# Three exchanges in the written order of a fused attention and token-mixing kernel, with seven PSUM homes moved

## The chip, the cores and the metric

The kernel runs on one core of a Trainium2 chip. A core has five engines that run their own instruction streams and meet only through semaphores: TensorE (PE, matrix products and transposes; PEld is its weight load), VectorE (DVE), ScalarE (ACT), GpSimd (POOL) and SyncE (SP), which here issues every DMA transfer. The metric is the device time of one execution in microseconds. All times inside an execution count from the first instruction of the profiled span.

## The reference

Inputs q, k and v are [8 batches, 8 heads, 576 positions, 64], and there are three weights. A linear attention with cosine and sine weights is followed by a mixing of the tokens:

```python
theta = np.pi / 2.0 * pos / S
def phi(x, c, s):
    r = np.maximum(x, 0.0)
    return np.concatenate([r * c, r * s], axis=-1)
q_p = phi(q, cos_w, sin_w); k_p = phi(k, cos_w, sin_w)
kv = np.einsum('bhsf,bhsd->bhfd', k_p, v)
z = np.sum(k_p, axis=2)
num = np.einsum('bhsf,bhfd->bhsd', q_p, kv)
den = np.einsum('bhsf,bhf->bhs', q_p, z)[..., None] + 1e-06
x = (num / den)                      # heads put side by side: [8, 576, 512]
...
W_tok = scale * np.einsum('bsd,btd->bst', x @ w_q, x @ w_k)
mixed = np.einsum('bst,btd->bsd', W_tok, x)
out = np.maximum(mixed, 0.0) @ w_out
```

## The kernel before

Work is cut into 16 halves: half H is four heads of batch H // 2. Nothing is scheduled by a compiler. One string, `ORDER` (lines 26 to 67), lists all steps as words, and lines 555 to 568 emit them one after the other; each engine gets its own steps in that sequence and works through them strictly in order. A word is a step, its number, sometimes a or b for one part of it, then `:n` for its home, the first of the eight PSUM banks that it writes, or `@A`, `@V`, `@G` for ACT, DVE or POOL. For the evictions OE, `:n` is one of 16 output buffers in SBUF instead.

The steps that matter below, for half H, batch b, row tile i:

- LK, LQ, LV (SP, line 145): load raw k, q, v. RK, RQ (lines 203, 205): relu and cast to bf16. VS (DVE, line 234) or VG (POOL, line 248): v times the cosine and sine table.
- QT H (PE, line 295, nine transposes of 128x128): q turned, into two banks (homes n and n+1). QM H (DVE, line 316, two instructions): the turned q times its table, from PSUM to SBUF; it empties QT's home.
- KV H (PE, line 285, 36 products): k'v; KE empties it into SBUF.
- N g (PE, line 340, 20 products; g is 2H or 2H+1): numerator and denominator from QM and KE, two banks. EP, RC or RJ: the reciprocal. X g (DVE, line 393): the quotient x; it empties N's home.
- XR H (PE, line 419, 20 transposes): x turned, two banks. XE H (line 213 on DVE, 209 on ACT) empties it.
- WK b, WQ b, KX b (PE, lines 439, 452, 466): the small products of the mixing, emptied by KW, QW, XK; XA and XB copy parts of XK's result across partitions.
- MX i (PE, line 489): one quarter of the mixed tokens of a batch, two banks. ME i (line 500 on ACT, 502 on DVE): relu, into SBUF.
- WO i (PE, line 509, four products of 128x512): a row tile of the product with w_out, one bank. OE i (line 209 on ACT, 213 on DVE): from PSUM into an output buffer. ST i (SP, line 519): store.

A step that writes a home waits until whatever stood there has been emptied. So the number after the colon is a dependency: QT12 in home 0 holds banks 0 and 1 until QM12 has read them, and the next step in home 0 waits for QM12. Buffers of most SBUF tiles alternate between two (`rq0`, `rq1`), raw inputs between five. SP works through loads and stores in one queue in the order of the string: a store whose eviction is late holds up the loads written behind it.

Of the kernel before, what the change touches and what calls it, by code (L numbers as in the profile page):

```python
# [39 lines left out]
CV8a@G KX2:7 LV9a KE6@A CW4@G X15 CW2@A N13:2 LK9a CW3@A CW5@V N12:0 EP13@V XR7:4 XK2@V LK8b WO8:6  # L40
RC13 XA2@A X13 EP12@A CV8b@G LK9b XE7@A WO2:7 RC12 VS8 LV11a WO7:2 CV9b@A RQ8a@G X12 OE8:0@A MX8:4
WO6:3 RQ8b@A RK8a@G LQ13a ME8@V OE7:1@A LQ11b XR6:0 RQ9a@G LQ10a WO1:6 CV9a@A XE6@V RQ9b@G LK11b
OE2:2@A WO4:2 LK11a VS9 OE6:3@A LQ11a RK8b@A QT9:0 RK9a@G OE1:4@A WK3:3 LV11b QM9 QT8:4 RK9b@G KW3@A
OE4:5@A KV8:0 QM8 XB2@A KV9:6 ST4 KE8@A LV12a MX9:4 KE9@A MX11:0 VG11a N16:2 ME9@A LK10a ME11@V
WQ3:6 RC16 LQ10b KX3:7 X16 QW3@A MX10:0 LV10a XK3@A N17:4 ME10@A N19:2 RK11@V N18:6 LV10b EP19@A
WO11:0 EP17@V RQ11@A LQ12a RC17 EP18@V X17 WO5:1 VG11b OE11:6@V WO10:4 OE5:5@A RC19 RC18 ST11 X18
WO9:5 LK12a X19 LK10b QT11:6 LQ13b OE9:7@A RQ10@G LV12b KV11:2 XA3@A QM11 XR8:0 LK12b KE11@A XR9:6
VG10a XE8@A QT10:2 LQ12b XE9@V WO0:5 QM10 OE10:8@A MX13:0 OE0:6@A MX12:6 N22:2 WO12:4 RQ13a@G ME12@V
EP22@A LV15a XB3@A ME13@A LV13a RC22 VG10b WK4:5 X22 LQ14b LV14b MX14:0 KW4@A N23:6 ME14@V LQ14a
MX15:2 EP23@A KX4:5 RK10@A LV13b WQ4:0 XK4@V RQ13b@G RC23 WO3:1 ME15@A X23 XA4@G XB4@A QW4@A RQ12b@G  # L50
KV10:2 OE3:9@V RQ12a@A QT13:6 OE12:10@A VG12 MX18:0 WO14:5 QM13 KE10@A ST12 ME18@A LK13b XR11:2
OE14:11@A LK13a MX16:0 N21:6 XE11@V ME16@A LV14a N20:4 EP21@A EP20@V RK12@A QT12:0 RJ10 X21 WO16:2
RQ14b@A X20 WO13:3 QM12 VG13 XR10:4 OE13:10@A MX19:6 KV12:0 ME19@A ST13 WO17:3 OE16:12@A LK15b
KE12@V XE10@V LK14b MX17:0 LK14a OE17:13@A N25:6 ME17@V N24:4 LV15b RQ14a@A WK5:3 ST2 EP25@V EP24@V
RK13@A RJ12 QT14:0 X24 WO21:2 KW5@A X25 CV14a@G KV13:4 OE21:10@A QM14 CV14b@A WQ5:3 ST21 KE13@A
KX5:2 LQ15b VS14 LQ15a XR12:4 XK5@A N27:0 ST3 XE12@A N26:6 LK15a RK14a@G WO20:2 RC26 EP27@V RC27
# [542 lines left out]
```

## Time and profile before

| | |
|---|---|
| time, median of 3 runs | 120.47 us |
| lowest and highest run | 119.94 and 120.84 us |
| profiled execution: span from first to last instruction | 117.9 us (its own time is not listed apart from the three) |
| PE, busy share of the span | 96.3 us, 82% |
| DVE | 91.0 us, 77% |
| ACT | 82.7 us, 70% |
| POOL | 64.8 us, 55% |
| transfers | 39.38 MB, 334 GB/s over the span |
| chain that ended last, by engine | PE 46%, DMA 25%, DVE 9%, SP's queue 8%, ACT 4% |

The shares are averages over stages with different limits. Rows of the timeline give the start, the duration, engine, line and operation, then out<-in by the program's names, the shapes and a count; a bracket at the end is the idle time of the engine before it and who ended it. Consecutive instructions of one line are merged into one row, so four WO in a row show as one row with x16. A row of the chain has a start, a duration and what it was.

### The profile page before, as it was taken

Reading aid. Unit: us, or ns where it says so; the run is one execution under the profiler, and the core shown is the slowest. Engines: PE = TensorE matmul, PEld = TensorE weight load, DVE = VectorE, ACT = ScalarE, POOL = GpSimd, SP = SyncE. Lnnn points to the kernel's source line nnn. Section 1 sums busy time; section 2 is a strip of 40 time slices with the busy share of each in tenths; the row PEclk is TensorE's granted clock in tenths of the full one; section 3 lists DMA queues with packets and bytes.
Section 4 is the critical chain, followed back from the end, with each engine's and each line's share of the span. In section 5 each row is a group of like instructions: output and inputs, shape, how many; then the busy total and the mean of one; then the engine's idle time right before and its main releaser. Section 6 shows DMA issues by size and latency. Waiting matters only on the chain.

```text
span 117.9 us, 4967 instructions
## 1 busy us (share of the span) xinstructions
PE 96.3 (82%) x2109; PEld 65.3 (55%) x2109; DVE 91.0 (77%) x163; ACT 82.7 (70%) x146; POOL 64.8 (55%) x66
## 2 busy tenths in 40 slices
PE   0007866887897879998999889997999999999970
PEld 0006855756676768546966556654784566463420
DVE  2009799699899998989798887796997996794620
ACT  4555578489999797997684769975888783546340
POOL 7600599843435984584599972899549921102000
PEclk9999999999999999999999999999999999999998
DMA  3999999999999999999999899786989456999874
GB/s 95 353 389 408 393 363 351 391 389 396 385 393 389 391 385 387 389 395 384 387 381 341 271 317 379 274 253 215 299 285 321 171 205 268 402 343 402 340 306 172
DMA packets 20662, 39.38 MB, mean 334 GB/s; under 512 B 3232, under 2 KB 3232, under 8 KB 20640
## 3 DMA queue, kind: packets, MB, share of 16 engines
q1 hardware_dynamic: 20640, 39.07, 91.8%
q8 instruction: 16, 0.26, 1.0%
q14 instruction: 6, 0.05, 0.1%
HBM read 29.62 MB, written 9.44 MB: 331 GB/s over the span
## 4 chain that ended last, share of the span: by engine, by line
PE 46%; DMA 25%; DVE 9%; SPq 8%; ACT 4%; issue 3%; POOL 2%; POOLq 0%; DVEq 0%
PE ps L509 23%; DMA kraw<-in_k_dram 11%; DMA vraw<-in_v_dram 9%; SPq L145 8%; DMA qraw<-in_q_dram 5%; DVE qm L316 5%; PE ps L340 4%; PE ps L452 3%; PE ps L466 3%; PE ps L489 3%; PE ps L439 3%; PE ps L285 3%; PE ps L419 2%; PE ps L295 2%; POOL rq L205 2%
## 5 line engine op out<-in xcount | busy, mean ns | idle before, releaser
L248 POOL TENSOR_TENSOR v<-vraw,vtab 128x1152 bf16<-128x1152 f32 (+1 forms) x12 | 35.6, 2976 | 4.5 <-DVE qm L316 2.5
L509 PE MATMUL ps<-wow,mix 128*128 128x512 bf16 x144 | 34.6, 380 | 0.0
L393 DVE TENSOR_TENSOR x<-ps,rec 128x640 bf16<-128x640 f32 x32 | 25.4, 816 | 0.7
L209 ACT COPY o<-ps 128x512 f32<-128x512 f32 x25 | 14.6, 590 | 10.5 <-PE ps L509 9.2
L316 DVE TENSOR_TENSOR qm<-ps,qtab 128x1152 bf16<-128x1152 bf16 x28 | 19.7, 749 | 1.3 <-PE ps L295 1.2
L509 PEld LDWEIGHTS <-mix 128*128 128x128 bf16 x144 | 12.5, 98 | 14.5 <-issue 1.7
L295 PE MATMUL ps<-ident,rq 128*128 128x128 bf16 x126 | 10.3, 232 | 10.9 <-ACT rq L203 10.0
L234 DVE TENSOR_TENSOR v<-vb,vtab 128x2304 bf16<-128x2304 bf16 (+1 forms) x11 | 12.0, 1110 | 7.5 <-ACT vb L209 6.7
L500 ACT ACTIVATE mix<-ps 128x576 bf16<-128x576 f32 x23 | 14.5, 651 | 2.5 <-PE ps L489 2.3
L340 PE MATMUL ps<-kvs,qm 64*128 64x65 bf16 x640 | 14.0, 193 | 2.8 <-DVE qm L316 1.8
L340 PEld LDWEIGHTS <-qm 64*128 64x128 bf16 x640 | 12.6, 96 | 4.9 <-issue 3.3
L295 PEld LDWEIGHTS <-rq 128*128 128x128 bf16 x126 | 8.2, 104 | 12.5 <-issue 9.9
L203 ACT ACTIVATE rk<-kraw 128x1152 bf16<-128x1152 f32 (+1 forms) x14 | 13.9, 995 | 0.5 <-DMA kraw<-in_k_dram 0.3
L211 POOL TENSOR_SCALAR kx<-kx 64x256 bf16<-64x256 bf16 x10 | 4.0, 400 | 15.8 <-ACT kx L209 10.1
L205 POOL TENSOR_SCALAR rq<-qraw 128x576 bf16<-128x576 f32 (+1 forms) x13 | 10.1, 776 | 4.4 <-ACT rk L203 2.6
L211 POOL TENSOR_SCALAR vb<-vraw 128x576 bf16<-128x576 f32 (+1 forms) x7 | 5.7, 809 | 10.8 <-DMA vraw<-in_v_dram 9.5
L285 PE MATMUL ps<-v,rk 64*64 64x130 bf16 x432 | 9.1, 228 | 1.9 <-ACT mix L500 0.7
L209 ACT CAST kvs<-ps 128x260 bf16<-128x260 f32 (+1 forms) x15 | 6.5, 436 | 5.1 <-PE ps L285 3.8
L285 PEld LDWEIGHTS <-rk 64*64 64x64 bf16 x432 | 7.5, 112 | 4.3 <-ACT mix L500 1.3
L502 DVE TENSOR_SCALAR mix<-ps 128x576 bf16<-128x576 f32 x9 | 6.8, 753 | 3.3 <-PE ps L489 3.1
L213 DVE COPY xT<-ps 128x1280 bf16<-128x1280 bf16 (+1 forms) x9 | 7.3, 813 | 2.2 <-PE ps L419 2.0
L203 ACT ACTIVATE rq<-qraw 128x576 bf16<-128x576 f32 (+1 forms) x10 | 8.3, 830 | 0.9 <-DMA qraw<-in_q_dram 0.8
(65 smaller groups left out, 135.0 us busy)
## 6 DMA issues: line engine op xcount, KB each, us to landing
kraw<-in_k_dram SPq DMA_DIRECT2D x32, 288.0 KB, 5.9
qraw<-in_q_dram SPq DMA_DIRECT2D x32, 288.0 KB, 5.9
vraw<-in_v_dram SPq DMA_DIRECT2D x32, 288.0 KB, 5.9
out_dram<-o SPq DMA_DIRECT2D x36, 256.0 KB, 3.0
wof<-in_moe_w_out_dram SPq DMA_DIRECT2D x4, 256.0 KB, 5.7
wkf<-in_moe_w_k_dram SPq DMA_DIRECT2D x1, 128.0 KB, 6.7
wqf<-in_moe_w_q_dram SPq DMA_DIRECT2D x1, 128.0 KB, 6.5
```

What stands on the lines that cost most here:

```text
L203: A.activation(dst, s, AF.Relu)
L205: eng.tensor_scalar(dst, s, FMAX, 0.0, op0=ALU.min, op1=ALU.max)
L209: A.copy(dst, s)
L234: V.tensor_mul(v2_b[H % NV2][:, part, :, :, 0:D], vb_b[H % NPREP][:, part].unsqueeze(3).to_broadcast([P, n, C, 2, D]), vtab.unsqueeze(1).t ...
L248: G.tensor_mul(dst[:, part, :, :, 0:D], s[:, part].unsqueeze(3).to_broadcast([P, n, C, 2, D]), vtab.unsqueeze(1).to_broadcast([P, n, C, 2, ...
L285: nc.tensor.matmul(kv_v[o, r, :], rk_of(H)[a, pr, c, :], v2_b[H % NV2][a, pr, c, :, 0:D + 1], start=(c == 0), stop=(c == C - 1))
L295: nc.tensor.transpose(qt_v[:, c, :], rq_b[H % NPREP][:, c, :, :], ident)
L316: V.tensor_mul(qm_b[H % NQM][:, :, r, 0:C, :], q_t[:, r].unsqueeze(1).to_broadcast([P, 2, C, H2]), qtab)
L340: nc.tensor.matmul(nv[:, pr, u, :], qm_b[H % NQM][a, s, r, 2 * u:2 * u + 2, :], kv_b[H % 2][a, r, pr if H in KV_WIDE else 0, s, 0:D + 1], ...
L393: V.tensor_tensor(x_b[b % NX][:, :, 4 * h:4 * h + 4, :].rearrange("p u (w r) d -> p r w u d", r=2)[:, r], nv[:, :, :, 0:D], rec(g).to_broa ...
L500: A.activation(dst, s, AF.Relu, scale=scale_moe)
L509: nc.tensor.matmul(o, mix_b[bp % 2][:, m, rt * P:(rt + 1) * P], wow[:, m, :], start=(m == 0), stop=(m == NDM - 1))
```

## The change

Only the string changes. Three pairs of steps change places, and seven numbers of homes are new: QT11 6 to 4, WO9 5 to 0, WO10 4 to 1, XR8 0 to 6, XR9 6 to 4, KV12 0 to 6, MX19 6 to 0. The order of the steps on DVE, ACT, POOL and SP stays as it was.

```diff
-OE2:2@A WO4:2 LK11a VS9 OE6:3@A LQ11a RK8b@A QT9:0 RK9a@G OE1:4@A WK3:3 LV11b QM9 QT8:4 RK9b@G KW3@A
+OE2:2@A QT8:4 LK11a VS9 OE6:3@A LQ11a RK8b@A QT9:0 RK9a@G OE1:4@A WK3:3 LV11b QM9 WO4:2 RK9b@G KW3@A
...
-RQ14b@A X20 WO13:3 QM12 VG13 XR10:4 OE13:10@A MX19:6 KV12:0 ME19@A ST13 WO17:3 OE16:12@A LK15b
+RQ14b@A X20 WO13:3 QM12 VG13 XR10:4 OE13:10@A KV12:6 MX19:0 ME19@A ST13 WO17:3 OE16:12@A LK15b
```

The second exchange stands on lines 46 and 47 of the string: `WO5:1 VG11b OE11:6@V WO10:4 OE5:5@A ... WO9:5 ... QT11:6` becomes `WO5:1 VG11b OE11:6@V QT11:4 OE5:5@A ... WO9:0 ... WO10:1`, with XR8 and XR9 on the same line.

First place, TensorE ahead of KV8. The names are bf16 tiles in SBUF: mix_104 the mixed tokens (WO), rq_81 and rq_80 the q of halves 9 and 8 (QT), xT_97 the turned x (WK), rk_78 and v_84 the k and v of half 8 (KV8). A bracket names the engines whose semaphores the instruction waits for. Before:

```order
L509 MATMUL ps<-wow,mix_104 128x512 [waits Activation_49]
...
L295 LDWEIGHTS rq_81 [waits Pool_49]
L295 MATMUL ps<-ident,rq_81 128x128 [waits DVE_49]
...
L439 MATMUL ps<-wkw,xT_97 128x64 [waits Activation_49]
...
L295 LDWEIGHTS rq_80
L295 MATMUL ps<-ident,rq_80 128x128
...
L285 MATMUL ps<-v_84,rk_78 64x130 [waits DVE_49]
```

And after the change:

```order
L295 LDWEIGHTS rq_80 [waits Activation_49,Pool_49]
L295 MATMUL ps<-ident,rq_80 128x128 [waits DVE_49]
...
L295 LDWEIGHTS rq_81 [waits Pool_49]
L295 MATMUL ps<-ident,rq_81 128x128 [waits DVE_49]
...
L439 MATMUL ps<-wkw,xT_97 128x64 [waits Activation_49]
...
L509 MATMUL ps<-wow,mix_104 128x512
...
L285 MATMUL ps<-v_84,rk_78 64x130 [waits DVE_49]
```

WO4 moved from ahead of both q transposes and WK3 to just ahead of KV8, and QT8 took its place.

Second place, TensorE from WO5 to KV11: mix_104 and mix_105 are the two buffers of mixed tokens (WO5 uses 104, WO10 and WO9 use 105), rq_81 is the q of half 11 (QT11), rk_79 and v_85 are KV11's. Before:

```order
L509 MATMUL ps<-wow,mix_104 128x512
...
L509 MATMUL ps<-wow,mix_105 128x512 [waits DVE_49]
...
L295 LDWEIGHTS rq_81 [waits Activation_49]
L295 MATMUL ps<-ident,rq_81 128x128 [waits DVE_49]
...
L285 LDWEIGHTS rk_79 [waits DVE_49]
L285 MATMUL ps<-v_85,rk_79 64x130 [waits Pool_49]
```

And after the change:

```order
L509 MATMUL ps<-wow,mix_104 128x512
...
L295 LDWEIGHTS rq_81 [waits Activation_49]
L295 MATMUL ps<-ident,rq_81 128x128 [waits DVE_49]
...
L509 MATMUL ps<-wow,mix_105 128x512 [waits DVE_49]
...
L509 MATMUL ps<-wow,mix_105 128x512 [waits Activation_49]
...
L285 LDWEIGHTS rk_79 [waits DVE_49]
L285 MATMUL ps<-v_85,rk_79 64x130 [waits Pool_49]
```

QT11 now stands ahead of the two WO, and the second of these waits for an eviction on ACT (bank 1, emptied by OE5). Further on, WO0 has a wait for DVE that it did not have (bank 5, emptied by XE9).

Third place, TensorE from MX19 (kx_102) and KV12 (rk_78, v_84) to MX17 (kx_102 again, behind WO17). Before:

```order
L489 LDWEIGHTS kx_102
L489 MATMUL ps<-wq_100,kx_102 128x288 [waits Activation_49]
...
L285 LDWEIGHTS rk_78 [waits DVE_49,Activation_49]
L285 MATMUL ps<-v_84,rk_78 64x130 [waits Pool_49]
...
L509 MATMUL ps<-wow,mix_105 128x512 [waits Activation_49]
...
L489 MATMUL ps<-wq_100,kx_102 128x288 [waits DVE_49]
```

And after the change:

```order
L285 LDWEIGHTS rk_78 [waits Activation_49]
L285 MATMUL ps<-v_84,rk_78 64x130 [waits Pool_49]
...
L489 LDWEIGHTS kx_102
L489 MATMUL ps<-wq_100,kx_102 128x288 [waits DVE_49]
...
L509 MATMUL ps<-wow,mix_105 128x512 [waits Activation_49]
...
L489 MATMUL ps<-wq_100,kx_102 128x288 [waits Activation_49]
```

KV12 moved ahead of MX19, and the wait for DVE (QM12, which empties home 0) went from KV12 to MX19.

More of the change, by code (lines that the diff above doesn't have):

```diff
@@ L42 @@
 WO6:3 RQ8b@A RK8a@G LQ13a ME8@V OE7:1@A LQ11b XR6:0 RQ9a@G LQ10a WO1:6 CV9a@A XE6@V RQ9b@G LK11b
-OE2:2@A WO4:2 LK11a VS9 OE6:3@A LQ11a RK8b@A QT9:0 RK9a@G OE1:4@A WK3:3 LV11b QM9 QT8:4 RK9b@G KW3@A
+OE2:2@A QT8:4 LK11a VS9 OE6:3@A LQ11a RK8b@A QT9:0 RK9a@G OE1:4@A WK3:3 LV11b QM9 WO4:2 RK9b@G KW3@A
 OE4:5@A KV8:0 QM8 XB2@A KV9:6 ST4 KE8@A LV12a MX9:4 KE9@A MX11:0 VG11a N16:2 ME9@A LK10a ME11@V
 WQ3:6 RC16 LQ10b KX3:7 X16 QW3@A MX10:0 LV10a XK3@A N17:4 ME10@A N19:2 RK11@V N18:6 LV10b EP19@A
-WO11:0 EP17@V RQ11@A LQ12a RC17 EP18@V X17 WO5:1 VG11b OE11:6@V WO10:4 OE5:5@A RC19 RC18 ST11 X18
-WO9:5 LK12a X19 LK10b QT11:6 LQ13b OE9:7@A RQ10@G LV12b KV11:2 XA3@A QM11 XR8:0 LK12b KE11@A XR9:6
+WO11:0 EP17@V RQ11@A LQ12a RC17 EP18@V X17 WO5:1 VG11b OE11:6@V QT11:4 OE5:5@A RC19 RC18 ST11 X18
+WO9:0 LK12a X19 LK10b WO10:1 LQ13b OE9:7@A RQ10@G LV12b KV11:2 XA3@A QM11 XR8:6 LK12b KE11@A XR9:4
 VG10a XE8@A QT10:2 LQ12b XE9@V WO0:5 QM10 OE10:8@A MX13:0 OE0:6@A MX12:6 N22:2 WO12:4 RQ13a@G ME12@V
```

## The prediction

> **What bounds the kernel now.** I read three views in this order: busy time by stretch, the idle places of TensorE from 50 us on, and the chain of waits. The first has, after each stretch, the busy time and instruction count of PE, PEld, DVE, ACT and POOL, then the granted clock, the DMA share and the GB/s.
>
> ```profile
> 31.00:57.30 26.30, 23.59 (x547) 17.63 (x548) 24.70 (x42) 23.11 (x43) 14.94 (x19) 1.00 1.05 389
> 57.30:80.67 23.37, 21.63 (x475) 14.13 (x475) 19.61 (x34) 18.11 (x35) 19.74 (x11) 1.00 0.91 314
> 80.67:114.30 33.63, 33.59 (x633) 19.39 (x633) 25.66 (x44) 20.35 (x38) 12.67 (x12) 1.00 0.84 300
> ```
>
> From 80.67 to 114.30 PE is busy 33.59 of 33.63 us: whatever brings PE to 80.67 earlier ends the kernel earlier, if the other engines and the transfers follow. From 57.30 to 80.67 PE has 1.74 us free. The timeline of PE from 50 to 115 us names an idle place over 0.15 us only four times:
>
> ```profile
> 56.01 1.25 PE L285 MATMUL ps<-v,rk 64*64 64x130 bf16 x72 [0.43 <-DVE qm L316]
> 66.04 0.47 PE L419 MATMUL ps<-ident,x 64*128 64x64 bf16 x20 [0.47 <-DVE qm L316]
> 68.75 0.48 PE L340 MATMUL ps<-kvs,qm 64*128 64x65 bf16 x20 [0.42 <-DVE qm L316]
> 80.67 0.72 PE L285 MATMUL ps<-v,rk 64*64 64x130 bf16 x36 [0.71 <-ACT mix L500]
> ```
>
> These are KV8 (with KV9 behind it), XR9, N22 and KV12, 2.03 us in all. Each waits for a q product (QM9, QM11, QM10, QM12) to leave PSUM or to be ready; the releaser that the last row names is corrected below. The three exchanges lie just ahead of them.
>
> **The change part by part.** No instruction is added or removed, and the order on DVE, ACT, POOL and SP is the same. So I walk PE's new order with start-to-start times from the old one, and let each step wait for what it needs.
>
> *First exchange (QT8 before QT9, WO4 after WK3).* Old rows:
>
> ```profile
> 52.10 1.90 PE L509 MATMUL ps<-wow,mix 128*128 128x512 bf16 x8
> 52.95 1.35 DVE L234 TENSOR_TENSOR v<-vb,vtab 128x2304 bf16<-128x2304 bf16 x1
> 53.83 0.67 PE L295 MATMUL ps<-ident,rq 128*128 128x128 bf16 x9
> 54.34 0.75 PE L439 MATMUL ps<-wkw,xT 128*128 128x64 bf16 x20
> 54.54 2.75 DVE L316 TENSOR_TENSOR qm<-ps,qtab 128x1152 bf16<-128x1152 bf16 x4 [0.24 <-PE ps L295]
> 54.92 0.67 PE L295 MATMUL ps<-ident,rq 128*128 128x128 bf16 x9
> 55.44 0.59 ACT L209 COPY o<-ps 128x512 f32<-128x512 f32 x1
> 57.34 0.42 PE L489 MATMUL ps<-wq,kx 64*128 64x288 bf16 x4
> ...
> out_dram<-o SPq DMA_DIRECT2D x1, 256.0 KB, 4.0
> ```
>
> The first row is WO1 and WO4: (53.83 - 52.10) / 2 = 0.87 each. QT9 takes 0.51 to the next start (54.34 - 53.83), WK3 0.58 (54.92 - 54.34). New: QT8 at 52.97, QT9 53.48, WK3 53.99, WO4 54.57, PE ready for KV8 at 55.44. QT9 ends at 53.48 + 0.67 = 54.15, so QM9 no longer waits for it but only for VS9 on its own engine, which ends at 54.30. DVE instructions in a row start some 0.05 before the last one's end, so QM9 starts at 54.25 instead of 54.54: 0.29 earlier. The fifth row is QM9 and QM8 without a gap; both move by 0.29, to an end at 57.00. KV8, held by QM9, moves by 0.29 to 55.72; MX9, held by QM8 (57.29, its start was 57.34), moves by 0.29 as well. More than 0.29 cannot be had here, because VS9 is now what QM9 waits for.
> What WO4's move costs: OE4 (seventh row) starts at 55.64 instead of 55.44. Behind it on ACT stand XB2 and the drain KE8, which then runs to about 57.0; MX11 needs it at 57.17, so 0.15 of cover is left. On SP the store ST4 and the six loads behind it go 0.20 later. The last row is ST4: 4.0 us from issue to landing, so transfers are queued ahead and 0.20 us is not seen. Cost 0; were the cover gone, 0.2.
>
> *Second exchange (QT11 ahead of WO9 and WO10, four homes changed).* Old rows:
>
> ```profile
> 60.39 3.63 PE L509 MATMUL ps<-wow,mix 128*128 128x512 bf16 x16
> 60.39 1.15 ACT L203 ACTIVATE rq<-qraw 128x1152 bf16<-128x1152 f32 x1
> 62.46 1.56 DVE L393 TENSOR_TENSOR x<-ps,rec 128x640 bf16<-128x640 f32 x2
> 63.86 0.67 PE L295 MATMUL ps<-ident,rq 128*128 128x128 bf16 x9
> 64.56 1.42 DVE L316 TENSOR_TENSOR qm<-ps,qtab 128x1152 bf16<-128x1152 bf16 x2 [0.54 <-PE ps L295]
> 65.10 0.47 PE L419 MATMUL ps<-ident,x 64*128 64x64 bf16 x20
> 65.61 1.23 ACT L209 COPY xT<-ps 128x1280 bf16<-128x1280 bf16 x1
> 66.44 0.68 PE L295 MATMUL ps<-ident,rq 128*128 128x128 bf16 x9
> 66.54 0.82 DVE L213 COPY xT<-ps 128x1280 bf16<-128x1280 bf16 x1 [0.56 <-PE ps L419]
> 66.95 1.03 PE L509 MATMUL ps<-wow,mix 128*128 128x512 bf16 x4
> 67.28 1.41 DVE L316 TENSOR_TENSOR qm<-ps,qtab 128x1152 bf16<-128x1152 bf16 x2
> ```
>
> All of it first moves by the 0.29 just gained, as PE runs without a wait from 57.34 to 66. The first row is WO11, WO5, WO10, WO9: (63.86 - 60.39) / 4 = 0.87. New: WO11 60.10, WO5 60.97, QT11 61.84 (its input RQ11, the second row, is ready at 61.54 - 0.29 = 61.25; its home 4 was left by X17, which ends before X18 starts at 62.46 - 0.29), ending at 62.51. WO9 goes at 62.35, WO10 at 63.22, KV11 at 64.09, XR8 at 64.7. WO9's new home 0 must be drained by OE11, which stands before X18 on DVE and so ended before 62.17: no wait. QM11 now only follows X19 (third row, end 64.02 - 0.29 = 63.73) instead of waiting 0.54 for QT11: it runs 63.68 to 65.10, 0.88 earlier. XR9 in its new home 4 needs it and starts at 65.15 instead of 66.04; PE's idle 0.47 there all but goes, since PE is ready at about 65.05.
> Then a new wait. XR9 fills banks 4 and 5, so WO0 in bank 5 must wait for XE9. XR9 ends at 65.62, XE9 runs 65.66 to 66.48, WO0 starts at 66.53 where PE was ready at 65.15 + 0.40 (66.44 - 66.04) + 0.51 = 66.06: a wait of 0.47, WO0 only 0.42 earlier than 66.95. Queued behind WO0 are MX13, MX12 and N22, and N22 waits for QM10 anyway. QM10 follows XE9 on DVE and moves with it: 66.40 instead of 67.28, 0.88 earlier, ending at 67.81; N22 starts at 67.87 instead of 68.75. PE reaches N22 at 66.53 + (68.75 - 0.42 - 66.95 = 1.38) - about 0.1 = 67.8 at the latest. So the new wait lies beside one that was there, and costs 0. MX13 now also waits for OE10 behind XE8 on ACT: XE8 starts with XR8's end at about 65.25, ends at 66.5, OE10 (0.59, like OE4) at 67.1; MX13 goes at 67.5. Sum at N22: 0.29 + 0.59 = 0.88.
>
> *Third exchange (KV12 ahead of MX19, homes swapped).* Old rows:
>
> ```profile
> 74.34 4.57 POOL L248 TENSOR_TENSOR v<-vraw,vtab 128x2304 bf16<-128x2304 f32 x1 [0.39 <-PE ps L285]
> 79.11 1.41 DVE L316 TENSOR_TENSOR qm<-ps,qtab 128x1152 bf16<-128x1152 bf16 x2
> 79.37 0.47 PE L419 MATMUL ps<-ident,x 64*128 64x64 bf16 x20
> 79.67 0.29 PE L489 MATMUL ps<-wq,kx 64*128 64x288 bf16 x2
> 80.00 0.65 ACT L500 ACTIVATE mix<-ps 128x576 bf16<-128x576 f32 x1
> 80.54 0.58 ACT L209 COPY o<-ps 128x512 f32<-128x512 f32 x1
> 81.32 1.04 PE L509 MATMUL ps<-wow,mix 128*128 128x512 bf16 x4
> 82.40 0.58 ACT L209 COPY o<-ps 128x512 f32<-128x512 f32 x1 [1.27 <-PE ps L509]
> 83.14 0.76 PE L439 MATMUL ps<-wkw,xT 128*128 128x64 bf16 x20
> ```
>
> KV12 sat in home 0, where QT12 had been: it waited for QM12 (second row, end 80.52), not for ME19, which no step of KV12 reads. In old times (the 0.88 comes off all of it): KV12 in home 6 starts after XR10 at 79.67, as v for it (first row, end 78.91) is there, and takes 0.65 (81.32 - 80.67). PE is ready for MX19 at 80.32; home 0 holds it until QM12 ends, start 80.57. WO17 follows about 0.15 later at 80.72 instead of 81.32. ME19 now starts at 80.91 instead of 80.00 and ends at 81.56; OE16 behind it at 82.05, OE17 at 82.54 instead of 82.98. WK5, whose bank OE17 empties, starts at 82.59 instead of 83.14: 0.55. The longer wait of ACT for MX19 takes 0.05 of the 0.60.
>
> *Sum.* 0.29 + 0.59 + 0.55 = 1.43, taken as 1.4. Bounds: QM9's start between 54.25 and 54.40 (an ordinary PE-to-DVE hand-over in place of the back-to-back one) gives 0.29 to 0.14; the third between 0.45 and 0.60. So 1.1 to 1.5 if all is passed on, and 1.4 is nearest to the measured hand-overs.
>
> A rule that speaks against this: the stretch row at 31 us shows 389 GB/s. The Trainium skill, "DMA: Bandwidth & Descriptors", Specifications, puts the HBM limit of a core at about 358 GB/s; by it 26.30 us at 389 would take 28.6 us (an estimate from that page), loads would be late everywhere and the lead worth nothing. The measured 389 GB/s is above that limit, so I do not take it as this run's bound.
> The clock: all three stretches have 1.00. The Trainium skill, "TensorE: Matmul & The Clock Gate", "A second HAM failure mode: psum-queue depth-cycling", says that short idles between groups can drop the clock, by which removing four of them would add to the gain; this case's clock shows no such drop, so I add nothing.
>
> **The rivals.**
>
> ```profile
> 68.66 4.64 DMA vraw<-in_v_dram
> 73.30 0.66 POOL rq L205
> ...
> 79.47 0.59 ACT L209 COPY o<-ps 128x512 f32<-128x512 f32 x1 [0.69 <-PE ps L509]
> ...
> DMA to landing us min/median/max: 2.0/3.0/5.9
> ```
>
> *Loads set the middle.* The chain of waits (first two rows) runs at 68.66 through a load of v into RQ12 on POOL. If that is real, the second exchange's 0.59 is lost there; SP moves by only 0.29, with ST11 behind OE11. Gain 0.29 + 0.55 = 0.84: 119.6. Against it: RQ12 reads q, not v, so the link looks like a coincidence of times.
> *Transfers set the end.* If 300 GB/s is all that the queue yields after 80.67, the last store cannot use the third exchange, and of the rest between 0.29 (SP's gate) and 0.88 passes; middle 0.58: 119.9. For it: stores take 3.0 us to land in the median against 2.0 at best (last row), so a queue stands. Against it: the same queue gave 389. [...]
> *Slower.* OE13 (third row) writes the same slot of o as OE12 and needs ST12 landed. ST12 is issued with OE12's end, 0.88 earlier; if its landing stays, OE13 ends at 79.8, when WO17, whose bank OE13 empties, wants to start (80.72 - 0.88 = 79.84). Each us later holds PE one us, and the loads behind ST13 too. ST12 took 4.0 us (the same row as ST4's). PE is later than before once OE13 ends after 81.27, that is, once ST12 takes some 6.4 us; the worst store took 5.9. Past that point by 1.0: 121.5.
>
> **How the numbers follow.** The median of the three runs is 120.47, the profiled span 117.9, so 2.57 lie around it; the execution's own time is not listed apart. Likeliest: span 116.5, time 120.47 - 1.4 = 119.07, say 119.1, chance 0.60. Loads in the middle 0.17, transfers at the end 0.17, slower 0.06. The range goes from 118.6 (a gain of 1.5, and the 0.4 by which the highest run lies off the median) to 120.1 (past both middle rivals), leaving out the slow one and the rivals' tails. One per cent, about what a measurement can tell from no change, is 1.2 us: 119.27. Of the likeliest case some four fifths lie below it (0.48). Within one per cent: its rest and the two middle rivals, 0.48. Slower by over one per cent: 0.04, most of the slow case.
>
> **What would show it.** First step right: KV8's idle gone or near 0.3, QM9 starting as VS9 ends. Second: QM11 without idle before it, XR9 too, and a new idle of some 0.5 before WO0, released by XE9. Third: KV12 right behind XR10, idle of about 0.2 before MX19, QM12 its releaser. N22 0.9 and WK5 1.4 earlier, PE's end at 112.9 instead of 114.3. Wrong would be: WK5 earlier by 1.4 but the last store not (transfers), or RQ12 unmoved (loads).

## The result and the profile after

The kernel before takes 120.73 us and the changed one 119.13 us (medians of six runs each on one chip). The ratio is 0.9891, with a 95% interval of 0.9857 to 0.9925. In a second set of runs, beside before again, it was 118.91 against 120.29 us, ratio 0.9880 (0.9837 to 0.9924). The change is faster by about 1.1%. Some executions were slower as a whole (121.77 us among the six of before, 189.75 us in the profiled one of the first exchange alone), and the ratios leave such runs out, as this text leaves out that one trace.

The profiled execution of the changed kernel has a span of 117.4 us, only 0.5 less than that of before. So I compare stretches between fixed places in the program: from XR6 to KV8 (first exchange), from KV8 to N22 (second), from N22 to WK5 (third), and on to the end of the last eviction. The columns are those of the prediction's stretches: window, its length, then the busy times. First before, then after, then the same changed kernel profiled a second time (after, again).

```profile
51.70:56.01 4.31, 3.88 (x67) 2.82 (x67) 3.59 (x6) 3.64 (x8) 2.25 (x3) 1.00 1.05 387
56.01:68.75 12.74, 11.77 (x297) 8.22 (x297) 10.95 (x21) 8.72 (x17) 11.18 (x6) 1.00 0.99 344
68.75:83.14 14.39, 13.58 (x333) 8.72 (x333) 11.61 (x19) 11.40 (x23) 11.03 (x6) 1.00 0.86 288
83.14:114.89 31.75, 31.12 (x556) 17.76 (x551) 23.99 (x42) 19.73 (x37) 10.20 (x12) 1.00 0.83 303
```

```profile
52.32:56.50 4.18, 3.83 (x66) 2.73 (x67) 3.67 (x5) 3.54 (x8) 2.53 (x4) 1.00 1.01 346
56.50:68.83 12.33, 11.76 (x294) 8.12 (x296) 10.79 (x20) 8.72 (x17) 8.83 (x5) 1.00 1.02 372
68.83:82.72 13.89, 13.28 (x332) 8.99 (x333) 11.63 (x19) 11.63 (x24) 12.57 (x7) 1.00 0.83 286
82.72:114.38 31.66, 30.52 (x550) 17.66 (x551) 24.06 (x42) 19.81 (x37) 10.66 (x12) 1.00 0.84 310
```

```profile
52.60:56.58 3.98, 3.83 (x66) 2.73 (x67) 3.47 (x5) 3.24 (x8) 2.21 (x3) 1.00 1.05 389
56.58:68.68 12.10, 11.60 (x294) 8.08 (x296) 10.80 (x20) 8.81 (x17) 9.84 (x6) 1.00 1.01 369
68.68:82.57 13.89, 13.27 (x331) 8.97 (x333) 11.63 (x19) 11.63 (x24) 11.84 (x6) 1.00 0.82 290
```

Each of the three stretches is shorter, and the last is not longer. In the first profile of after they give 0.13 + 0.41 + 0.50 = 1.04 us, in the second 0.33 + 0.64 + 0.50 = 1.47. The spans show less because the executions had gone differently before that: up to XR6 the code is the same, yet QT1, the first transposes, came at 9.60 us before and at 10.04 and 10.17 after, and XR6 at 51.70 before and at 52.32 and 52.60 after.

TensorE's timeline of the changed kernel (first profile) at the three places, and at the end two rows of DVE from the second profile, QM9 with QM8 and QM11; a row has start, duration, line, tiles, shapes, count, and in brackets an idle time with its releaser:

```profile
55.39 0.81 PE L509 MATMUL ps<-wow,mix 128*128 128x512 bf16 x3
56.50 1.25 PE L285 MATMUL ps<-v,rk 64*64 64x130 bf16 x72 [0.30 <-DVE qm L316]
...
62.62 0.89 PE L295 MATMUL ps<-ident,rq 128*128 128x128 bf16 x9
63.35 1.89 PE L509 MATMUL ps<-wow,mix 128*128 128x512 bf16 x8
65.17 0.72 PE L285 MATMUL ps<-v,rk 64*64 64x130 bf16 x36
65.82 0.76 PE L419 MATMUL ps<-ident,x 64*128 64x64 bf16 x40
66.51 0.68 PE L295 MATMUL ps<-ident,rq 128*128 128x128 bf16 x9
67.50 1.02 PE L509 MATMUL ps<-wow,mix 128*128 128x512 bf16 x3 [0.31 <-DVE xT L213]
68.46 0.42 PE L489 MATMUL ps<-wq,kx 64*128 64x288 bf16 x4
68.83 0.48 PE L340 MATMUL ps<-kvs,qm 64*128 64x65 bf16 x20
...
79.46 0.47 PE L419 MATMUL ps<-ident,x 64*128 64x64 bf16 x20
79.86 0.72 PE L285 MATMUL ps<-v,rk 64*64 64x130 bf16 x36
80.67 0.30 PE L489 MATMUL ps<-wq,kx 64*128 64x288 bf16 x2
80.90 1.04 PE L509 MATMUL ps<-wow,mix 128*128 128x512 bf16 x3
...
55.11 2.75 DVE L316 TENSOR_TENSOR qm<-ps,qtab 128x1152 bf16<-128x1152 bf16 x4
64.50 1.41 DVE L316 TENSOR_TENSOR qm<-ps,qtab 128x1152 bf16<-128x1152 bf16 x2
```

WO4 now stands ahead of KV8, which still waits 0.30 us for QM9. QT11 comes ahead of WO9 and WO10; XR8 and XR9 run as one row of x40 without the idle of 0.47; the new wait is at WO0, 0.31 us for XE9; N22's idle is gone. KV12 follows XR10, MX19 follows KV12. On DVE neither QM9 nor QM11 has an idle in front of it any more. One row is odd: QT11 takes 0.89 us, where before each such QT took 0.66 to 0.68.

### The profile page after: what moved, and what is told of

It reads as the page before. It is cut to its first block, busy times and chain, and to the rows that moved or that the text cites. A ratio compares the mean times of both kernels' runs of the same rounds, so it can differ in the third digit from the quotient of the medians.

```text
span 117.4 us, 4953 instructions
## 1 busy us (share of the span) xinstructions
PE 94.9 (81%) x2095; PEld 64.9 (55%) x2109; DVE 90.9 (77%) x163; ACT 82.8 (71%) x146; POOL 65.3 (56%) x66
## 4 chain that ended last, share of the span: by engine, by line
PE 50%; DVE 28%; DMA 9%; issue 4%; ACT 4%; POOL 1%; SPq 1%; DVEq 0%; ACTq 0%; POOLq 0%
PE ps L509 24%; DVE qm L316 12%; DVE x L393 7%; PE ps L340 5%; DMA vraw<-in_v_dram 5%; DMA qraw<-in_q_dram 4%; DVE v L234 4%; PE ps L489 4%; PE ps L439 3%; PE ps L285 3%; PE ps L466 3%; PE ps L452 3%; PE ps L419 3%; DVE xT L213 3%; ACT rk L203 1%
## 5 line engine op out<-in xcount | busy, mean ns | idle before, releaser
L509 PE MATMUL ps<-wow,mix 128*128 128x512 bf16 x130 | 33.1, 380 | 1.3 <-issue 0.5
L509 PEld LDWEIGHTS <-mix 128*128 128x128 bf16 x144 | 12.5, 98 | 14.4 <-issue 1.7
L205 POOL TENSOR_SCALAR rq<-qraw 128x576 bf16<-128x576 f32 (+1 forms) x13 | 11.3, 869 | 6.1 <-ACT rk L203 2.8
L203 ACT ACTIVATE rk<-kraw 128x1152 bf16<-128x1152 f32 (+1 forms) x14 | 13.9, 994 | 0.6 <-DMA kraw<-in_k_dram 0.6
```

The lines of the kernel that those rows point to most:

```text
L203: A.activation(dst, s, AF.Relu)
L205: eng.tensor_scalar(dst, s, FMAX, 0.0, op0=ALU.min, op1=ALU.max)
L509: nc.tensor.matmul(o, mix_b[bp % 2][:, m, rt * P:(rt + 1) * P], wow[:, m, :], start=(m == 0), stop=(m == NDM - 1))
```

## The experiments

The edits are to the string and, for four kernels, to the loads. "Whole loads" means that all loads are as before.

### One exchange at a time

```diff
# x1_alone, x1_again
-OE2:2@A WO4:2 LK11a VS9 OE6:3@A LQ11a RK8b@A QT9:0 RK9a@G OE1:4@A WK3:3 LV11b QM9 QT8:4 RK9b@G KW3@A
+OE2:2@A QT8:4 LK11a VS9 OE6:3@A LQ11a RK8b@A QT9:0 RK9a@G OE1:4@A WK3:3 LV11b QM9 WO4:2 RK9b@G KW3@A
# x2_alone
-WO11:0 EP17@V RQ11@A LQ12a RC17 EP18@V X17 WO5:1 VG11b OE11:6@V WO10:4 OE5:5@A RC19 RC18 ST11 X18
-WO9:5 LK12a X19 LK10b QT11:6 LQ13b OE9:7@A RQ10@G LV12b KV11:2 XA3@A QM11 XR8:0 LK12b KE11@A XR9:6
+WO11:0 EP17@V RQ11@A LQ12a RC17 EP18@V X17 WO5:1 VG11b OE11:6@V QT11:4 OE5:5@A RC19 RC18 ST11 X18
+WO9:0 LK12a X19 LK10b WO10:1 LQ13b OE9:7@A RQ10@G LV12b KV11:2 XA3@A QM11 XR8:6 LK12b KE11@A XR9:4
# x3_alone
-RQ14b@A X20 WO13:3 QM12 VG13 XR10:4 OE13:10@A MX19:6 KV12:0 ME19@A ST13 WO17:3 OE16:12@A LK15b
+RQ14b@A X20 WO13:3 QM12 VG13 XR10:4 OE13:10@A KV12:6 MX19:0 ME19@A ST13 WO17:3 OE16:12@A LK15b
```

> The first exchange alone (QT8 and WO4). Theory, each exchange shortens PE's path by itself and what it gains is passed to the end: from XR6's start to KV8's start 4.31 us before become 4.0 to 4.2 (the kernel with all three showed 4.18, where VS9 took 1.55 us instead of 1.35), KV8 to N22 stays 12.74, N22 to WK5 stays 14.39; time 0.1 to 0.3 us below before. Rival, loads set the stretch up to the middle: XR6 to KV8 shorter, but the same amount comes back between KV8 and N22 and the time is that of before within 0.1.

> The second exchange alone (QT11 ahead of WO9 and WO10, with its homes). Theory: KV8's start to N22's start 12.74 us before become 12.15 to 12.35, the longer value if QT11 shows the stall of 0.23 behind its first transpose as with all three; the other two stretches as before; time 0.4 to 0.6 us below before. Rival, loads set the middle: RQ12 on POOL stays where it was and N22 to WK5 grows by what was gained; time as before within 0.1.

> The third exchange alone (KV12 ahead of MX19, homes 6 and 0). Theory: N22's start to WK5's start 14.39 us before become 13.85 to 13.9, the stretches before it stay, WK5 to the last eviction stays 31.2 to 31.75 as in the two kernels; time 0.5 to 0.6 us below before. Rival, transfers set the end: N22 to WK5 shorter, but the last eviction or the last store comes later against WK5 by as much; time as before within 0.2.

Measured, with the 95% interval of the ratio to before: first exchange 1.0003 (0.9968 to 1.0037), second 0.9958 (0.9922 to 0.9995), third 0.9957 (0.9922 to 0.9992). So the first was worth nothing that shows, though its interval still holds the 0.1 to 0.3 us expected, and the others 0.5 us each. The traces speak against both rivals. With the second exchange alone N22 to WK5 was 14.41 us, not longer by what had been gained, so loads did not take it back. With the third alone WK5 to the last eviction was 31.67 against 31.75, so transfers did not take it back either. The first was run and profiled once more.

> First exchange alone (QT8 and WO4 changed), profiled a second time. Theory (QM9 starts as VS9 ends): from XR6's start to KV8's start 4.0 to 4.2 us instead of 4.31, N22 as much earlier and no more, so a time of -0.1 to -0.3 us (ratio 0.997 to 0.999). Rival (the lead is lost again in the waits for QM11 and QM10, which stand behind VG11, loads and evictions): the stretch to KV8 is shorter, the one from KV8 to N22 longer by the same, ratio 1.000.

Measured: ratio 0.9985 (0.9957 to 1.0014). The stretches of this run, then TensorE's weight loads at KV8 and KV9 (the bracket named issue is a stop in which no semaphore is waited for):

```profile
51.77:55.75 3.98, 3.83 (x66) 2.73 (x67) 3.58 (x6) 3.24 (x8) 2.31 (x3) 1.00 1.05 392
55.75:68.94 13.19, 11.82 (x295) 8.15 (x297) 10.99 (x21) 9.04 (x17) 10.88 (x6) 1.00 1.02 363
68.94:83.52 14.58, 13.04 (x329) 8.72 (x333) 11.57 (x19) 11.55 (x23) 11.35 (x6) 1.00 0.81 276
```

```profile
55.90 0.76 PEld L285 LDWEIGHTS <-rk 64*64 64x64 bf16 x47
57.20 0.22 PEld L285 LDWEIGHTS <-rk 64*64 64x64 bf16 x12 [0.55 <-issue]
```

The first stretch is 0.33 shorter, as the theory had it. But TensorE stops in KV9, which is merged with KV8 here, between two products of one line that wait for nothing, and the second stretch is 0.45 longer than before; the third is 0.19 longer. The other two kernels had such a stop as well. In the third exchange alone it stood in WO10, far ahead of what was changed:

```profile
60.65 2.33 PE L509 MATMUL ps<-wow,mix 128*128 128x512 bf16 x9
63.55 1.25 PE L509 MATMUL ps<-wow,mix 128*128 128x512 bf16 x5 [0.57 <-issue]
```

Its stretch from KV8 to N22 was 13.49 us in place of 12.74, while that from N22 to WK5 was 13.88, the full gain. In the second exchange alone the stop stood in KV9 again, and the stretch was 12.33.

### WO0 without its new wait

```diff
# e4_wo0: and every later home 0, 1 and 4, 5 of TensorE's steps changed over
-VG10a XE8@A QT10:2 LQ12b XE9@V WO0:5 QM10 OE10:8@A MX13:0 OE0:6@A MX12:6 N22:2 WO12:4 RQ13a@G ME12@V
+VG10a XE8@A QT10:2 LQ12b XE9@V WO0:0 QM10 OE10:8@A MX13:4 OE0:6@A MX12:6 N22:2 WO12:0 RQ13a@G ME12@V
```

> All three exchanges, with WO0 in bank 0 instead of 5 and, behind it, the bank pairs 0,1 and 4,5 swapped for every step, so that WO0 no longer waits for XE9. Theory, WO0's new wait lies beside N22's wait for QM10 and costs nothing: WO0 0.4 to 0.5 us earlier, N22 idle 0.3 to 0.5 before it, KV8 to N22 12.33 within 0.06, time that of the changed kernel within 0.2 (1.1 per cent below before). Rival, the new wait is paid: N22 and the end 0.3 to 0.5 us earlier than in the changed kernel, 1.4 per cent below before.

Measured: ratio 0.9909 (0.9876 to 0.9943), no better than the changed kernel. Four rows of its timeline: WO0 and N22 on TensorE, and the weight loads at WO14.

```profile
66.56 0.81 PE L509 MATMUL ps<-wow,mix 128*128 128x512 bf16 x3
...
68.14 0.49 PE L340 MATMUL ps<-kvs,qm 64*128 64x65 bf16 x20 [0.43 <-DVE qm L316]
```

```profile
74.05 0.11 PEld L509 LDWEIGHTS <-mix 128*128 128x128 bf16 x2
75.12 0.31 PEld L509 LDWEIGHTS <-mix 128*128 128x128 bf16 x2 [0.96 <-issue]
```

WO0 no longer waits, and N22 now waits for QM10 instead: the wait was only moved. KV8 to N22 is 12.09 us, 0.24 less than in the first profile of after, which looked like a gain; but the second profile of after has 12.10 with WO0's wait in it. And a stop of 0.96 us, named issue, stood inside WO14; N22 to WK5 took 14.61 instead of 13.89.

### What the stops are

The trace lists 16 transfers of 16 KB of a queue that it calls instruction, about 1 us each. All of these stops stood at weight loads number 989, 1117 and 1373 of the program (counted from 0), which are 128 and 256 apart; with its product each weight load is two instructions, so 128 of them are 256. TensorE's 2109 weight loads and as many products make 16.5 blocks of 256. My theory: these are TensorE's instructions; a block is asked for when TensorE comes to the end of the one before, and comes late when loads are in front of it. From the trace's transfer records, with the distance from the load before as it is in profiles without a stop as the usual one (us):

```
kernel, stop in                TensorE 128 loads   packet         new block   stop beyond the
                               earlier                            begins      usual distance
x1_again, KV9                  51.0                54.63-55.72    57.20       0.6
x2_alone, KV9                  51.4                55.13-56.25    57.58       0.4
x3_alone, WO10                 57.1                61.15-62.09    63.55       0.9
after, QT11                    57.3                60.67-61.60    62.91       0.2
before, WO14                   69.2                72.94-73.90    75.15       0.3
x1_again, WO14                 69.3                73.11-74.10    75.38       0.3
x2_alone, WO14                 69.1                72.70-73.59    74.97       0.1
e4_wo0, WO14                   68.6                72.90-73.88    75.12       0.8
after again, WO14              69.1                71.79-72.74    74.83       none
```

Each stop ended 1.24 to 1.48 us after the packet. In all the thirteen profiles used here, no block that began after 50 us did so sooner than 1.24 us after its packet's end, stop or not. To test the theory, four kernels with little left to load (three quarters of the columns of the late loads are left out, so the output is not the reference's):

```diff
         for r in (0, 1) if part is None else (part,):
-            nc.sync.dma_start(raw[nm][H % NRAW][:, r, :], src[nm][b][:, 2 * h + r, :])
+            w = HC // 4 if H >= 11 else HC
+            nc.sync.dma_start(raw[nm][H % NRAW][:, r, 0:w], src[nm][b][:, 2 * h + r, 0:w])
```

> The changed kernel, profiled a second time, to see which of its stretches repeat. Theory (a late packet of TensorE's instructions costs what the engine's waits do not explain): XR6 to KV8 4.0 to 4.2, KV8 to N22 12.1 to 12.4, N22 to WK5 13.9 us, save where one of the idles named issue shows, by whose length the stretch is longer. Rival (the difference between the sum and the measured gain is a wait for loads or evictions that moved): the stretches have other lengths without such an idle. Ratio 0.986 to 0.993 either way.

> The kernel before, in which every load of k, q and v from half 11 on brings only the first quarter of the columns, so the transfers have little left to do from about 50 us on (the rest of these buffers keeps older data, so the output is not the reference's). Theory (TensorE's order and the q products bound the middle): the idles ahead of KV8, XR9, N22 and KV12 stay as they were, stretches 4.3, 12.7 and 14.1 to 14.4 us, and the time is the same within 1 us. Rival (loads set the middle): the stretches from KV8 to WK5 shrink by over 1 us.

> The changed kernel with the same short loads from half 11 on (output not the reference's). Theory (late instruction packets behind the loads cost part of the gain): packets come within 1.5 us of being asked for, no idle named issue over 0.15 us at weight loads 1117 and 1373; stretches 4.0 to 4.2, 12.1 to 12.33 and 13.9 us, 1.2 to 1.5 us less than the kernel before with the same short loads. Rival (the stall belongs to the place in the program and not to the loads): the idle of 0.2 us in QT11 stays. Rival (transfers take back part of the gain): the difference to the kernel before grows past 1.6 us.

> The first exchange alone, with the same short loads from half 11 on (output not the reference's). With whole loads its lead of 0.33 us at KV8 was gone at N22, and inside KV8 stood a stop named issue. Theory (late instruction packet): 4.0 us from XR6 to KV8, 12.74 from KV8 to N22 as in the kernel before with short loads, 14.4 from N22 to WK5, so the lead of 0.33 reaches the end. Rival (the lead is waited away at QM11 or QM10): KV8 to N22 13.0 to 13.2 again.

> All three exchanges with WO0 in bank 0, and only the first quarter of the columns of every load from half 11 on (output not the reference's). With whole loads this order lost 1.00 us ahead of WO14, named issue, right where TensorE needs its next packet of instructions. Theory (the packet was late because the loads were in front of it): the packet comes within 1.5 us of being asked for, the idle is gone, N22 to WK5 13.9 us instead of 14.6, KV8 to N22 12.1. Rival (the stall belongs to this instruction or this order): the idle and 14.6 stay.

Measured: the numbers of after_again stand above, with 3.98, 12.10 and 13.89 us and no stop. Ratio to before with whole loads: before_thin 0.9988 (0.9962 to 1.0013), x1_thin 0.9973 (0.9952 to 0.9994), after_thin 0.9870 (0.9826 to 0.9915), e4_thin 0.9884 (0.9850 to 0.9918). Stretches of before_thin, after_thin, x1_thin and e4_thin:

```profile
52.28:56.59 4.31, 3.89 (x67) 2.82 (x67) 3.82 (x6) 3.80 (x8) 2.33 (x4) 1.00 0.82 267
56.59:69.33 12.74, 11.66 (x294) 8.21 (x296) 10.93 (x21) 8.74 (x17) 11.39 (x6) 1.00 0.73 221
69.33:83.74 14.41, 13.17 (x330) 8.86 (x333) 11.66 (x19) 11.41 (x23) 10.76 (x6) 1.00 0.30 84
```

```profile
52.63:56.76 4.13, 3.93 (x67) 2.77 (x67) 3.75 (x6) 3.77 (x9) 3.73 (x4) 1.00 0.81 243
56.76:68.86 12.10, 11.60 (x294) 8.10 (x296) 10.79 (x20) 8.77 (x17) 10.76 (x6) 1.00 0.71 223
68.86:82.75 13.89, 13.27 (x331) 8.98 (x333) 11.63 (x19) 11.63 (x24) 10.88 (x6) 1.00 0.30 86
```

```profile
52.29:56.27 3.98, 3.83 (x67) 2.73 (x67) 3.48 (x6) 3.24 (x8) 2.34 (x3) 1.00 0.65 204
56.27:69.01 12.74, 11.67 (x295) 8.22 (x296) 10.93 (x21) 9.13 (x17) 10.55 (x6) 1.00 0.68 210
69.01:83.41 14.40, 13.16 (x330) 8.86 (x333) 11.65 (x19) 11.41 (x23) 11.68 (x6) 1.00 0.33 92
```

```profile
52.51:56.81 4.30, 3.83 (x66) 2.74 (x67) 3.80 (x6) 3.66 (x8) 2.47 (x4) 1.00 0.71 218
56.81:68.92 12.11, 11.49 (x295) 8.06 (x297) 10.85 (x21) 8.92 (x17) 10.77 (x6) 1.00 0.71 217
68.92:82.80 13.88, 13.26 (x329) 8.97 (x332) 11.57 (x19) 11.31 (x23) 10.88 (x6) 1.00 0.31 89
```

Three things follow. First, before_thin moves 84 GB/s from N22 to WK5, where the kernel before moves 288, and each stretch has the length it had: loads do not set the middle. Second, the stops are gone in all four: no stretch from KV8 on has another length than 12.74 or 12.10, 14.4 or 13.9, with or without an exchange. x1_thin keeps its lead of 0.33 to the end, and e4_thin has 13.88 where whole loads gave 14.61. Over these thirteen profiles the packet that WO14 needs started 1.9 to 4.3 us after TensorE had passed the place before with whole loads (nine profiles), and 0.5 to 1.6 us after with short ones (four). Third, WO0's wait costs nothing: 12.10 with it, 12.11 without. After_thin lies 1.60 us below before_thin where 1.2 to 1.5 was expected and the rival began beyond 1.6; with these intervals the times don't tell, the stretches do: up to WK5 they sum to 31.46 us for before_thin and to 30.12 for after_thin, 1.34 less.

The first stretch of e4_thin, 4.30 us, is a miss of another kind. VS9 on DVE and RK9a on POOL, in after again (DVE, then POOL) and in e4_thin (the same):

```profile
53.85 1.35 DVE L234 TENSOR_TENSOR v<-vb,vtab 128x2304 bf16<-128x2304 bf16 x1
...
52.92 0.67 POOL L205 TENSOR_SCALAR rk<-kraw 128x576 bf16<-128x576 f32 x1
```

```profile
53.76 1.67 DVE L235 TENSOR_TENSOR v<-vb,vtab 128x2304 bf16<-128x2304 bf16 x1
...
53.55 0.67 POOL L206 TENSOR_SCALAR rk<-kraw 128x576 bf16<-128x576 f32 x1 [0.16 <-DMA kraw<-in_k_dram]
```

Where RK9a has ended before VS9 starts, VS9 takes 1.35; where RK9a still runs, VS9 is longer. In e4_thin a load of k made RK9a start late (the bracket). It ends at 55.43, which is 1.21 after RK9a's end (54.22); in the first profile of after it is 1.55, from 53.57 to 55.12, again 1.21 after RK9a's end (53.91); and in before_thin 1.60, 1.21 after it. So the first stretch is 3.98, 4.18 or 4.30 by when RK9a runs. In after_thin it is 4.13 for another reason: VS9 began 0.15 later after XE6 than elsewhere, right behind the end, at 53.98, of the cast on ACT that makes its input.

### Making the packet come earlier, and filling N22's idle

```diff
# e6_loads, on top of e4_wo0 (e5_loads: and "WO12:0 N22:2" in place of "N22:2 WO12:0")
-EP22@A LV15a XB3@A ME13@A LV13a RC22 VG10b WK4:1 X22 LQ14b LV14b MX14:4 KW4@A N23:6 ME14@V LQ14a
-MX15:2 EP23@A KX4:1 RK10@A LV13b WQ4:4 XK4@V RQ13b@G RC23 WO3:5 ME15@A X23 XA4@G XB4@A QW4@A RQ12b@G
+EP22@A XB3@A ME13@A LV13a RC22 VG10b WK4:1 X22 LV13b LQ14b MX14:4 KW4@A N23:6 ME14@V
+MX15:2 EP23@A KX4:1 RK10@A WQ4:4 XK4@V RQ13b@G RC23 WO3:5 ME15@A X23 XA4@G XB4@A QW4@A RQ12b@G
...
-OE14:11@A LK13a MX16:4 N21:6 XE11@V ME16@A LV14a N20:0 EP21@A EP20@V RK12@A QT12:4 RJ10 X21 WO16:2
+OE14:11@A LK13a MX16:4 N21:6 XE11@V ME16@A LV14a LV14b LQ14a LV15a N20:0 EP21@A EP20@V RK12@A QT12:4 RJ10 X21 WO16:2
```

> All three exchanges with WO0 in bank 0, full loads, and three loads moved behind the loads that follow ST12: first part of q and second of v of half 14, first part of v of half 15; the second part of v of half 13 goes ahead of q of half 14 instead. At the place where TensorE asks for the packet that WO14 needs, three loads instead of five are in the queue. Theory (the queue ahead of the packet sets when it comes): the packet 1 to 2 us sooner, no stop of 1.0 us ahead of WO14, N22 to WK5 13.9 to 14.1; ratio to the kernel before 0.984 to 0.990. Rival (the packet's time is chance, or its engine is shared whatever is queued): a stop named issue in some other place or the same, ratio about 0.991 as without the move.

> As the kernel with the three loads moved, and WO12 goes ahead of N22, into the idle of 0.43 us in which N22 waits for QM10. Theory (TensorE is the bound there): N22 0.3 us later, everything from WK4 on 0.4 us earlier, ratio 0.003 below that of the kernel with the loads moved. Rival (the chain from N22 by EP22, X22 and XR11 to the q products is the bound): WK5 no earlier, the idle shows ahead of MX19 or KV12 instead, ratio the same within 0.003.

Measured: e6_loads 0.9951 (0.9926 to 0.9976), e5_loads 1.0005 (0.9968 to 1.0041). Both are slower than the changed kernel; of the versions that compute the whole result none beats it. Two rows of e6_loads, then two of e5_loads, on TensorE:

```profile
68.85 1.02 PE L509 MATMUL ps<-wow,mix 128*128 128x512 bf16 x4 [0.39 <-ACT o L209]
...
84.94 0.68 PE L295 MATMUL ps<-ident,rq 128*128 128x128 bf16 x9 [1.87 <-ACT rq L203]
```

```profile
70.64 1.02 PE L509 MATMUL ps<-wow,mix 128*128 128x512 bf16 x4 [0.32 <-ACT o L209]
...
73.42 0.30 PE L489 MATMUL ps<-wq,kx 64*128 64x288 bf16 x2 [0.65 <-ACT mix L500]
```

In e6_loads the packet started 3.4 us after its place was passed instead of 4.3 and there was no stop at WO14. But N22 to WK5 took 14.33 us where 13.9 to 14.1 was expected: WO12 waited 0.39 for OE0 (first row), and OE0 1.03 for the landing of ST11, a store that was issued ahead of all the moved loads. And LQ14a, one of the loads moved, now landed at 84.18; RQ14a waited for it, and QT14 for RQ14a, 1.87 us. (That profile is the longest of its twelve runs, 120.92 us; the median, 119.85, lost less. The profile of e5_loads is of a long run too, 123.15 us where the median is 121.09; in the stretches read here its clock was 1.00.) Since one profile shows one packet, a gain of 1.0 us may also be chance, as packets scatter from 1.9 to 4.3; what the profile of e6_loads shows is that LQ14a couldn't be moved that far. In e5_loads WO12 waits 0.32 for bank 0, and N22 comes later; EP22 waits for N22 on ACT, ME13 stands behind EP22, and MX14 needs ME13: an idle of 0.65. KV8 to WK5 is 26.70 us in place of the 26.44 of e6_loads, so the theory fell. The rival held in part: WK5 is no earlier, but the idle stands ahead of WO12 and MX14 instead of MX19 or KV12, and the ratio is 0.005 higher where it was to be the same within 0.003.

## Why the prediction was right

The time came out at 119.13 where 119.1 was predicted, and the ratio of 0.9891 lies near the 0.988 that 119.07 to 120.47 would be. That the time fits to 0.03 us is luck: the six runs put before 0.26 above the three that the prediction started from, and the interval of the ratio leaves a gain of 0.9 to 1.7 us. What bears the prediction out is the stretches. Point by point:

- *First exchange, 0.29.* The mechanism holds: QM9 now starts as VS9 ends (55.11 and 55.20 in after again), and the gain is 0.33 where VS9 takes 1.35 us. That is more than the 0.29 that was called the most, as QM9 starts 0.09 before VS9's end and not 0.05. The lower bound of 0.14 was too high and had the wrong reason: not the hand-over to QM9 but the length of VS9 is uncertain, and at 1.67 the gain is 0.01. That moving WO4 costs nothing is right (12.74 from KV8 to N22 in x1_thin, as in before_thin).
- *Second exchange, 0.59.* 0.64 in after again and with short loads. The wait at WO0 for XE9 was foretold, at 0.47; it measured 0.31, and as said it lies beside N22's wait for QM10.
- *Third exchange, 0.55.* 0.50 in every profile that has it and neither a stop nor a new wait in that stretch. KV12 follows XR10's start by 0.40, not 0.30, since I put it where MX19 had stood. That QM12, not ME19, held KV12 follows from the string of before, where ME19 stands behind KV12, and the trace agrees: KV12 now starts while QM12 still runs (79.20 to 80.61), and MX19, which took over home 0, starts 0.06 after QM12's end. The idle of 0.2 foretold there is too short to be shown.
- *The sum, 1.43.* 1.47 in after again. In the first profile of after 1.04 at WK5: 0.20 went to VS9's length and 0.23 to the stop in QT11. The prediction had no term for such stops. PE's end, foretold at 112.9, came at 113.76 and 113.61, since these executions had reached XR6 0.6 and 0.9 us later than that of before.
- *The base.* The prediction took 2.57 us to lie around the span. In the runs of after whose times and spans are listed together, it is 1.8 (119.19 and 117.4). So the profiled execution of before was a short one, about 119.7, and the span of 116.5 that I gave was 0.9 too low, though the time was not: it rested on the median less the gain.
- *Loads set the middle* fell with before_thin. *Transfers set the end* fell too: the last stretch is no longer (31.67 against 31.75), and with fewer bytes after_thin's was 31.67. *Slower, by OE13 waiting for ST12's landing*: OE13 waited for TensorE in both profiles of after, as before. Such a wait is real elsewhere: in e6_loads OE0 waited 1.03 us for ST11 to land.

How much a stop costs differs. Against the same stretches without a stop (12.74 or 12.10, 14.41 or 13.89), the stops of 0.6 and 0.4 us in KV9 cost 0.45 and 0.23, the 0.9 in WO10 0.75, the 0.2 in QT11 0.23 and the 0.8 in WO14 of e4_wo0 0.73. At the same place the 0.3 of x1_again cost 0.17 and the 0.3 of before nothing: there the products behind the late weight load came only 0.06 us later. In its profiled run such stops took back the whole lead of the first exchange. That this is why its times show nothing with whole loads, and why the terms measured one by one, 0, 0.5 and 0.5 us, do not add up to the 1.4 of the whole, is argued from single profiles and not shown. How much of it is chance in which run had a stop, the intervals of 0.3 to 0.4% leave open.

## What to carry to other kernels

An exchange in the order pays where a wait ends last, and what it pays is the distance to the next thing that holds the waiter: VS9 for the first, X19 for the second, about KV12's own length for the third (0.5 of 0.65 us). Compare profiles by stretches between fixed places, since two executions reached the same place up to 0.9 us apart, which is more than one exchange was worth. A new wait that lies beside an old one is free, and so is removing it.

## What the runs showed of the hardware

As far as the times tell, TensorE can stop for its own instructions. The Trainium skill, "Runtime: NRT & Kernel Launch", Instruction fetch mechanics, says that blocks of 16 KiB, 256 instructions, are fetched by the sequencer over a queue of its own while it works on the current one; the trace agrees with the 16 packets and the spacing. It calls the cost of crossing a block mostly hidden; here, in stretches with 276 to 372 GB/s of transfers, it was up to 0.9 us at one crossing, and from KV8 on it did not show with the short loads. That TensorE asks for a block as it ends the one before is inferred from the times; no record shows the asking, and with short loads four packets began up to 0.34 us before that place was passed, so the asking must come somewhat earlier.

DVE and POOL held each other up. In after_thin RK9a started at 54.01 and VS9 at 54.02, and this time VS9 kept its 1.36 us, and RK9a took 1.89 instead of 0.67 (the row has RK9a and RK9b):

```profile
54.02 1.36 DVE L235 TENSOR_TENSOR v<-vb,vtab 128x2304 bf16<-128x2304 bf16 x1
...
54.01 2.52 POOL L206 TENSOR_SCALAR rk<-kraw 128x576 bf16<-128x576 f32 x2 [0.17 <-DMA kraw<-in_k_dram]
```

The Trainium skill, "SBUF — State Buffer", Who interferes with whom, says that these two engines share a pair of ports as an exclusive lock. The ends agree: VS9, when late, ended a fixed 1.21 us behind RK9a's end three times. The other way round it is as fixed: in twelve of the thirteen profiles an RK on POOL ran at the same time as VS9 and outlasted it, and it ended 0.52 or 0.53 us after VS9's end each time.
